# The projection stage of a concat kernel (S4D convolution beside full attention): the seeds' work requested in small pieces between projections

## The chip, the cores and the metric

The kernel runs on one core of one Trainium2 chip, as one launch. The metric is the device time of that launch in microseconds; the median of three runs stands for the kernel.

## What is computed

Two results of shape 1 x 2048 x 448 are put side by side. The first is an S4D state-space convolution: a kernel K of length 2048 for each of 448 channels, from 256 complex modes each, convolved with u. The second is 16-head attention without a mask, with heads of 28.

```python
# A
dt = exp(log_dt); A = -exp(log_A_real) + 1j * A_imag; C = (C_real + 1j * C_imag) * dt[:, None]
P = exp((A * dt[:, None])[:, :, None] * pos[None, None, :])          # 448 x 256 x 2048
K = 2.0 * einsum("dn,dnl->dl", C, P).real
y = irfft(rfft(u_t, 2 * L) * rfft(K, 2 * L), 2 * L)[:, :, :L];  a = y + u * D_skip
# B
q, k, v = split(x @ wqkv);  p = softmax(q @ k.T * 28 ** -0.5);  b = (p @ v) @ wo
out = concatenate([a, b], axis=-1)
```

## The kernel before

The program has three stages.

**The projection stage** (0 to 206 us). The rows of x come in four chunks c of 512. For each chunk `transposes` turns x with TensorE (PE) into four pairs `xh`, `xl` (the value rounded to the matmul's format, by ScalarE (ACT), and the rest, by VectorE (DVE)). Then come twelve projections: eight of q and k (`qk_proj`, one for each of four groups of heads and each of the two) and four of v (`v_proj`); the last chunk has its v first. A projection is twelve matmuls into one of three PSUM buffers `pm`, taken in turn. `project()` issues one projection and then the evacuation of the one before: for q and k ACT writes the high half of `hl`, DVE the low half, and SyncE (SP) stores both; for k of the first two chunks ACT and DVE also form `kb`, and POOL a part of `dhl`. An evacuation of v is ACT's alone.

Between the projections stands work that has nothing to do with them: **the seeds** of the convolution, eight of them (`seeds(o)`, 56 of the 448 channels each). A seed has thirteen steps: `load` (four DMAs), `exp_a` and `times_dt` (ACT), `turn` (eight transposes on PE, a copy on ACT), `phases` (three short and one long instruction on DVE, one long on POOL), `reduce` (two long ones on DVE), `sines` (three long ones on ACT), `sizes` (one long on ACT) with `g_base` (POOL), `places` with the factors `fa` and `e_base` (DVE; POOL), `e3` and `g_first` (DVE, 6 and 9 instructions), the factors `fb` with `e5` and `g_copies` (DVE; POOL; ACT), and two stores. A long instruction has 128 x 1232 elements.

The steps go into slots: step i of seed o into slot 4o + i (`SP` = 4), `load` two slots early. There are 41 slots; the 48 projections are spread evenly over the first `PW` = 37, so that about 1.3 projections are requested, then one slot's steps in whole, then 1.3 projections again:

```python
for t in range(n_stage):
    while work and n_work - len(work) < n_work * (t + 1) / PW:
        project()
    for f in slots[t] + ahead.get(t, []):
        f()
```

After slot 36 the last evacuation is requested and then the loads of the stage to come; the last four slots, seed 7's end, follow.

In this stage nothing is kept in program order (`KEPT["p"]` is empty): the order of requests gives priorities, from which the framework's scheduler makes each engine's instruction order when the program is built. At run time each engine follows its fixed order.

**The bridge** (206 to 260 us): the first loads of k (`khat`), q (`qhat`) and v for attention, and the row maxima of the first unit.

**The main stage** (from 260 us): scores, exponentials and products with v, with the rest of the convolution in between, in an order written out by hand (`ORDER`), which the scheduler keeps.

Every engine instruction is issued through the wrapper `Kept`, so the profile gives line 75 for all of them; they are told apart by their tiles. In the seeds `tri` holds the phases (`r`), sines (`sn`) and sizes (`mg`); `pn` is the turned input in PSUM; `qhat` and `sg` are also the seeds' results; `px` is a PSUM buffer for products.

Of the kernel before, what the change touches and what calls it, by code (L numbers as in the profile page):

```python
# [8 lines left out]
F32 = mybir.dt.float32  # L9
# [3 lines left out]
ALU = mybir.AluOpType  # L13
# [10 lines left out]
HG = H // G  # L24
CQ = 512
NQ = L // CQ
# [64 lines left out]
def body(ctx, tc, a, out):  # L91
# [117 lines left out]
    with ExitStack() as st:  # L209
# [102 lines left out]
        def seeds(o):  # L312
# [23 lines left out]
            def phases():  # L336
                tri = t_p.tile([128, 3, LV, NH], F32, name="tri", bufs=2)
                q["r"], q["sn"], q["mg"] = r, sn, mg = tri[:, 0], tri[:, 1], tri[:, 2]
                t0, k0, im = sn[:, 0, :], sn[:, 1, :], q["ps"][:, 1].rearrange("p b h e -> p (b h e)")
                vec.tensor_scalar(k0, im, MAGIC, None, op0=ALU.add)  # L340
                vec.scalar_tensor_tensor(t0, k0, MAGIC, im, op0=ALU.subtract, op1=ALU.subtract)
                vec.tensor_scalar(t0, t0, 0.5, -0.5, op0=ALU.min, op1=ALU.max)
                mul(vec, r, lb(t0), kb)
                mul(pol, mg, lb(q["tr"]), kb)

            def reduce():
                vec.tensor_scalar(q["sn"], q["r"], MAGIC, MAGIC, op0=ALU.add, op1=ALU.subtract)
                vec.tensor_tensor(q["r"], q["sn"], q["r"], ALU.subtract)

# [29 lines left out]

            def g_first():  # L380

                c0 = q["ps"][:, 2:4].rearrange("p c b h e -> p c (b h e)")
                px = ps_x.tile([128, CQ], F32, name="px")
                c1, x_ = (px[:, i:i + 2 * NH].rearrange("p (c n) -> p c n", c=2) for i in (0, 2 * NH))
                g4_ = lambda e: q["sg"][:, :, :F_Z - F_G].rearrange("p b (c h e) -> p c b h e", c=2, e=4)[:, :, :, :, e]
                bh = lambda t: t.rearrange("p c (b h) -> p c b h", h=16)
                zr = lambda k: q["r"][:, 6 + k, :][:, None, :].to_broadcast([128, 2, NH])
                tt = vec.tensor_tensor
                for k, src, e, dst in ((0, c0, 1, bh(c1)), (1, c0, 2, g4_(2)), (1, c1, 3, g4_(3))):
                    tt(g4_(e), bh(src), bh(zr(k)), ALU.mult)  # L390
                    tt(x_, src[:, ::-1], q["gz"][:, k], ALU.mult)
                    tt(dst, g4_(e), bh(x_), ALU.add)
                q["c"] = c0, c1
# [5 lines left out]

            def factors(i, k, p_, n_):  # L400
                zz, mg = q["zz"], q["mg"]
                mul(vec, zz[:, i:i + 3, :, 0, :], vk(mg, k), vk(q["r"], k))
                mul(vec, zz[:, i:i + 3, :, p_, :], vk(mg, k), vk(q["sn"], k))
                for k in range(i, i + 3):
                    act.activation(zz[:, k, :, n_, :], zz[:, k, :, p_, :], AF.Copy, scale=-1.0)

            def cmul(e, dst, s0, n, wr, wi, conj):

# [4 lines left out]
                br, bi = (w_[:, :, :, None].to_broadcast([128, BO, 16, n]) for w_ in (wr, wi))  # L413
                for c in range(2):
                    mul(e, dst[c], s0[c], br)
# [4 lines left out]
            e8 = lambda *i: sl(q["e8"], *i)  # L420
            e3 = lambda: cmul(vec if o % 8 < E3 else pol, e8(3, 4), e8(1, 2), 1, q["e8"][:, :, 0, :, 2], q["e8"][:, :, 1, :, 2], False)
            e5 = lambda: cmul(pol, e8(5, 8), e8(1, 4), 3, q["e8"][:, :, 0, :, 4], q["e8"][:, :, 1, :, 4], False)
# [3 lines left out]
            def load():  # L426
                if o not in nats:
                    load_nat(o)
                q["nat"] = nats.pop(o)
            dts = lambda *r: [lambda i=i: times_dt(i) for i in r]  # L430
            fa, fb = lambda: factors(0, 3, 2, 1), lambda: factors(3, 8, 1, 2)
            return [[load], [exp_a] + dts(1, 2, 3), dts(0), [turn], [phases], [reduce], [sines], [sizes, g_base],
                    [places, fa, e_base], [e3, g_first], [fb, e5, g_copies], [put_g], [put_e]]

# [59 lines left out]

        work = []
        for c in range(NQ):
            jobs = [lambda c=c, s=s, g=g: qk_proj(c, s, g) for g in range(G) for s in (1, 0)]
            v_jobs = [lambda c=c, t=t: v_proj(c, t) for t in range(4)]
# [8 lines left out]
        for o in range(NO):  # L507
            for i, st_ in enumerate(stages[o]):
                slots[max(SP * o + (i or -2), 0)] += st_
        slots[1].insert(0, turn_dt)  # L510
        pend, n_work = [], len(work)
# [7 lines left out]
        def project():  # L519
# [4 lines left out]
            if e:  # L524
                pend.append(e)

        for t in range(n_stage):
            while work and n_work - len(work) < n_work * (t + 1) / PW:
                project()
            for f in slots[t] + ahead.get(t, []):  # L530
                f()
            if t + 1 == PW:
                project()
                wst.close()
                k0_p = pool(k0_st, "k0_p", side="right")
                for j in range(HG):
                    load_k(0, j, k0_p, nc.scalar if j < 2 else nc.sync)
                load_q(1)
                for c in range(NQ):
                    load_v(0, c)  # L540
        xst.close()
# [569 lines left out]
```

## Time and profile before

| | us |
|---|---|
| median of 3 runs (lowest, highest) | 1343.49 (1342.39, 1343.78) |
| the profiled execution | 1344.13 |
| its span, first to last instruction | 1342.4 |
| TensorE (PE), busy in the span | 1247.8 (93%) |
| VectorE (DVE) | 994.4 (74%) |
| ScalarE (ACT) | 953.5 (71%) |
| GpSimd (POOL) | 838.6 (62%) |

The shares are means over stages with different limits, so a change to one stage is read in that stage. Each row of the stretches gives the length, then the busy time and number of instructions of PE, of its weight loads (PEld), of DVE, ACT and POOL, then the granted TensorE clock, the share of the DMA engines and GB/s. A row of the chain of waits gives start, length and what the end waited for. A row of waits reads: who waited, for whom, in total, how often, the longest. A row of the timeline gives start, length, engine, tiles (out<-in), shape, and in brackets the idle time before it with what ended it. A row of the groups gives tiles, shapes and count, then busy time and the mean of one in ns, then idle time before. An engine named with a q (ACTq, SPq) is its sequencer, which issues DMAs.

### The profile page before, as it was taken

The numbers are of one execution on the slowest core, as the hardware profiler recorded it, in microseconds if no ns is written. First come the engines' busy times: TensorE is split into PE (matmuls) and PEld (weight loads), VectorE is DVE, ScalarE is ACT, GpSimd is POOL, SyncE is SP. The second block draws the span as 40 slices with busy tenths as digits, with TensorE's granted clock in tenths as the row PEclk, the third lists the DMA queues.
The fourth block names the chain that finished last, engine by engine and source line by source line (L and its number), as shares of the span: only waits on it lengthen the run. The fifth ranks groups of instructions, "written<-read, shape, count | busy, mean of one in ns | idle before, by whom it ended". The sixth has DMA issues, their size and how long they took to land.

```text
span 1342.4 us, 33143 instructions
## 1 busy us (share of the span) xinstructions
PE 1247.8 (93%) x12625; PEld 706.7 (53%) x12625; DVE 994.4 (74%) x2138; ACT 953.5 (71%) x2067; POOL 838.6 (62%) x705
## 2 busy tenths in 40 slices
PE   7879885899999999999999999999998899998998
PEld 5657762355555555555555555555554445544433
DVE  5897786877777777787788888988886757757311
ACT  4876762488888788888888888888885556645552
POOL 3685681187878877878889989989983202112221
PEclk9879886899999999999999999999998999999999
DMA  6677669626765556478633314641424444635476
GB/s 196 209 257 260 216 213 290 194 67 146 174 151 122 111 148 173 124 171 222 173 89 85 97 47 92 147 99 47 115 79 144 142 119 169 201 131 190 147 189 174
DMA packets 200088, 205.36 MB, mean 153 GB/s; under 512 B 95992, under 2 KB 158520, under 8 KB 197880
## 3 DMA queue, kind: packets, MB, share of 16 engines
q1 hardware_dynamic: 199544, 201.13, 54.0%
q10 hardware_dynamic: 384, 2.10, 0.5%
q8 instruction: 100, 1.64, 0.5%
q14 instruction: 60, 0.49, 0.1%
HBM read 120.73 MB, written 82.18 MB: 151 GB/s over the span
## 4 chain that ended last, share of the span: by engine, by line
PE 70%; DVE 13%; ACT 6%; DMA 4%; POOL 3%; issue 2%; SPq 1%; ACTq 0%; DVEq 0%; POOLq 0%
PE pm L75 39%; PE po L75 16%; PE pss L75 15%; DVE mx L75 2%; DVE tri L75 2%; ACT p L75 2%; DVE p L75 2%; DVE pr L75 1%; POOL qhat L75 1%; DMA khat<-k 1%; DVE sg L75 1%; DVE px L75 1%; DVE qhat L75 1%; ACT tri L75 1%; DMA q<-hl 1%
## 5 line engine op out<-in xcount | busy, mean ns | idle before, releaser
L75 ACT ACTIVATE p<-pss 128x512 f32<-128x512 f32 x1024 | 562.0, 612 | 142.1 <-PE pss L75 137.7
L75 PE MATMUL pss<-qhat,khat 128*128 128x512 f32 x1024 | 406.3, 403 | 7.0 <-ACT p L75 4.3
L75 DVE TENSOR_REDUCE mx<-pm 128x1 f32<-128x512 f32 x500 | 321.7, 684 | 117.7 <-PE pm L75 113.4
L75 PE MATMUL pm<-khat,qhat 128*128 128x512 f32 x749 | 328.5, 442 | 15.7 <-DVE mx L75 10.9
L75 POOL TENSOR_TENSOR e<-e,sdb 128x256 f32<-128x256 f32 x168 | 201.8, 1201 | 147.0 <-ACT e L75 138.1
L75 PE MATMUL po<-p,v 128*32 128x512 f32 x2048 | 272.4, 599 | 0.0
L75 POOL TENSOR_TENSOR e<-e,eu 128x256 f32<-128x256 f32 x168 | 248.2, 1478 | 13.2
L75 PEld LDWEIGHTS pm<-khat,qhat 128*128 128x128 f32 x749 | 142.6, 191 | 211.7 <-ACT p L75 43.6
L75 PEld LDWEIGHTS pss<-qhat,khat 128*128 128x128 f32 x1024 | 191.2, 189 | 64.1 <-ACT p L75 27.5
L75 DVE CUSTOM_DVE_ANT_0 rl<-pm,rl 128x512 f32<-128x512 f32 x249 | 171.7, 690 | 61.8 <-ACT rl L75 58.0
L75 POOL TENSOR_TENSOR eu<-e,sdb 128x256 f32<-128x256 f32 x168 | 202.0, 1202 | 0.0
L75 ACT ACTIVATE rl<-pm 128x512 f32<-128x512 f32 x249 | 151.5, 609 | 20.8 <-PE pm L75 18.3
L75 DVE TENSOR_TENSOR g<-g,zg 128x128 f32<-128x128 f32 x392 | 162.1, 414 | 4.2 <-ACT zg L75 0.8
L75 POOL TENSOR_TENSOR p<-pr,pr 64x448 f32<-64x448 f32 x32 | 40.9, 1277 | 197.4 <-DVE pr L75 186.4
L75 PE MATMUL pm<-kdif,qhat 128*128 128x512 f32 x249 | 101.6, 408 | 2.4 <-DMA v<-v 1.3
L75 DVE TENSOR_TENSOR zg<-g,zg 128x128 f32<-128x128 f32 x224 | 88.0, 393 | 5.1
L75 PEld LDWEIGHTS pm<-e,g 128*32 128x32 f32 x3584 | 57.4, 110 | 41.5 <-DVE mx L75 18.2
L75 PE MATMUL pm<-xh,wh 112*128 112x512 f32 x128 | 57.8, 456 | 20.9 <-DVE hl L75 9.7
L75 PE MATMUL pm<-e,g 128*32 128x64 f32 x3584 | 73.2, 222 | 0.0
L75 ACT ACTIVATE y<-pm 128x448 f32<-128x448 f32 x48 | 26.3, 548 | 65.6 <-PE pm L75 33.3
L75 PEld LDWEIGHTS po<-p,v 128*32 128x32 f32 x2048 | 56.0, 110 | 22.8 <-issue 18.3
L75 ACT ACTIVATE ub<-pm 128x224 f32<-128x224 f32 (+1 forms) x96 | 38.7, 448 | 39.4 <-PE pm L75 38.3
(137 smaller groups left out, 1575.1 us busy)
## 6 DMA issues: line engine op xcount, KB each, us to landing
sdb<-sd SPq DMA_DIRECT2D x56, 336.0 KB
qhat<-q SPq DMA_DIRECT2D x64, 256.0 KB
khat<-k SPq DMA_DIRECT2D x56, 256.0 KB
sd<-sg SPq DMA_DIRECT2D x8, 1456.0 KB
k<-hl SPq DMA_DIRECT2D x16, 512.0 KB
q<-hl SPq DMA_DIRECT2D x16, 512.0 KB
mw<-in_mw SPq DMA_DIRECT2D x16, 512.0 KB
sd<-qhat SPq DMA_DIRECT2D x8, 896.0 KB
```

The source lines that it names most:

```text
L75: i = f(*args, **kw)
```

## The change

The slots stay, but they are flattened into one queue of (weight, function). The weight is a constant for the DVE time of the piece, in us; steps with little or no DVE work have weight 0. Steps are cut: `phases` gives up its long instructions to `turns`; `reduce`, `e3` and the factors come in two parts, `g_first` in three. Each projection has an amount `took` of DVE time of its own: 0.7 for an evacuation of q or k, 1.1 where `kb` is formed, 0 for v, and 2.0 more where a chunk's transposes come. All weights and amounts together, divided by 48, give `each`; after every projection `due` grows by `each - took`, and pieces are taken from the queue while the next one's weight is not above `due`. A piece of weight 0 is taken at once. What is left in the queue after the 48th projection, and the slots from 37 on, follow as before. The instructions themselves are the same.

```diff
--- before.py
+++ after.py
@@ -340,12 +340,17 @@
                 vec.tensor_scalar(k0, im, MAGIC, None, op0=ALU.add)
                 vec.scalar_tensor_tensor(t0, k0, MAGIC, im, op0=ALU.subtract, op1=ALU.subtract)
                 vec.tensor_scalar(t0, t0, 0.5, -0.5, op0=ALU.min, op1=ALU.max)
-                mul(vec, r, lb(t0), kb)
-                mul(pol, mg, lb(q["tr"]), kb)
-
-            def reduce():
-                vec.tensor_scalar(q["sn"], q["r"], MAGIC, MAGIC, op0=ALU.add, op1=ALU.subtract)
-                vec.tensor_tensor(q["r"], q["sn"], q["r"], ALU.subtract)
+                q["t0"] = t0
+
+            def turns():
+                mul(vec, q["r"], lb(q["t0"]), kb)
+                mul(pol, q["mg"], lb(q["tr"]), kb)
+
+            def reduce(i):
+                if i == 0:
+                    vec.tensor_scalar(q["sn"], q["r"], MAGIC, MAGIC, op0=ALU.add, op1=ALU.subtract)
+                else:
+                    vec.tensor_tensor(q["r"], q["sn"], q["r"], ALU.subtract)
 
             def sines():
                 act.activation(q["sn"], q["r"], AF.Sin, scale=TWO_PI)
@@ -377,19 +382,21 @@
                 mul(pol, gz[:, :, 0], q["mg"][:, 6:8, :], q["sn"][:, 6:8, :])
                 act.activation(gz[:, :, 1], gz[:, :, 0], AF.Copy, scale=-1.0)
 
-            def g_first():
+            def g_first(i):
 
                 c0 = q["ps"][:, 2:4].rearrange("p c b h e -> p c (b h e)")
-                px = ps_x.tile([128, CQ], F32, name="px")
+                if i == 0:
+                    q["px"] = ps_x.tile([128, CQ], F32, name="px")
+                px = q["px"]
                 c1, x_ = (px[:, i:i + 2 * NH].rearrange("p (c n) -> p c n", c=2) for i in (0, 2 * NH))
                 g4_ = lambda e: q["sg"][:, :, :F_Z - F_G].rearrange("p b (c h e) -> p c b h e", c=2, e=4)[:, :, :, :, e]
                 bh = lambda t: t.rearrange("p c (b h) -> p c b h", h=16)
                 zr = lambda k: q["r"][:, 6 + k, :][:, None, :].to_broadcast([128, 2, NH])
                 tt = vec.tensor_tensor
-                for k, src, e, dst in ((0, c0, 1, bh(c1)), (1, c0, 2, g4_(2)), (1, c1, 3, g4_(3))):
-                    tt(g4_(e), bh(src), bh(zr(k)), ALU.mult)
-                    tt(x_, src[:, ::-1], q["gz"][:, k], ALU.mult)
-                    tt(dst, g4_(e), bh(x_), ALU.add)
+                k, src, e, dst = ((0, c0, 1, bh(c1)), (1, c0, 2, g4_(2)), (1, c1, 3, g4_(3)))[i]
+                tt(g4_(e), bh(src), bh(zr(k)), ALU.mult)
+                tt(x_, src[:, ::-1], q["gz"][:, k], ALU.mult)
+                tt(dst, g4_(e), bh(x_), ALU.add)
                 q["c"] = c0, c1
 
             def g_copies():
@@ -397,28 +404,29 @@
                     for e in range(2):
                         act.activation(q["g4"][:, :, c, :, e], q["c"][e][:, c].rearrange("p (b h) -> p b h", h=16), AF.Copy)
 
-            def factors(i, k, p_, n_):
+            def factors(i, k, p_, n_, imag):
                 zz, mg = q["zz"], q["mg"]
-                mul(vec, zz[:, i:i + 3, :, 0, :], vk(mg, k), vk(q["r"], k))
+                if not imag:
+                    return mul(vec, zz[:, i:i + 3, :, 0, :], vk(mg, k), vk(q["r"], k))
                 mul(vec, zz[:, i:i + 3, :, p_, :], vk(mg, k), vk(q["sn"], k))
                 for k in range(i, i + 3):
                     act.activation(zz[:, k, :, n_, :], zz[:, k, :, p_, :], AF.Copy, scale=-1.0)
 
-            def cmul(e, dst, s0, n, wr, wi, conj):
+            def cmul(e, dst, s0, n, wr, wi, conj, cs=(0, 1)):
 
                 if e is nc.vector:
                     x_ = ps_x.tile([128, CQ], F32, name="px")[:, :BO * 16 * n].rearrange("p (b h e) -> p b h e", h=16, e=n)
                 else:
                     x_ = s_p.tile([128, BO, 16, 4], F32, name="x_e")[:, :, :, :n]
                 br, bi = (w_[:, :, :, None].to_broadcast([128, BO, 16, n]) for w_ in (wr, wi))
-                for c in range(2):
+                for c in cs:
                     mul(e, dst[c], s0[c], br)
                     mul(e, x_, s0[1 - c], bi)
                     e.tensor_tensor(dst[c], dst[c], x_, ALU.add if (c == 0) == conj else ALU.subtract)
 
             sl = lambda t, i0, i1: [t[:, :, c, :, i0:i1] for c in range(2)]
             e8 = lambda *i: sl(q["e8"], *i)
-            e3 = lambda: cmul(vec if o % 8 < E3 else pol, e8(3, 4), e8(1, 2), 1, q["e8"][:, :, 0, :, 2], q["e8"][:, :, 1, :, 2], False)
+            e3 = lambda c: cmul(vec if o % 8 < E3 else pol, e8(3, 4), e8(1, 2), 1, q["e8"][:, :, 0, :, 2], q["e8"][:, :, 1, :, 2], False, (c,))
             e5 = lambda: cmul(pol, e8(5, 8), e8(1, 4), 3, q["e8"][:, :, 0, :, 4], q["e8"][:, :, 1, :, 4], False)
             put_e = lambda: nc.sync.dma_start(sd_d[o][:, :, :F_G].rearrange("b p f -> p b f"), q["se"])
             put_g = lambda: nc.sync.dma_start(sd_d[o][:, :, F_G:].rearrange("b p f -> p b f"), q["sg"])
@@ -428,9 +436,13 @@
                     load_nat(o)
                 q["nat"] = nats.pop(o)
             dts = lambda *r: [lambda i=i: times_dt(i) for i in r]
-            fa, fb = lambda: factors(0, 3, 2, 1), lambda: factors(3, 8, 1, 2)
-            return [[load], [exp_a] + dts(1, 2, 3), dts(0), [turn], [phases], [reduce], [sines], [sizes, g_base],
-                    [places, fa, e_base], [e3, g_first], [fb, e5, g_copies], [put_g], [put_e]]
+            fa, fb = ([(0.75, lambda a_=a_, i=i: factors(*a_, i)) for i in range(2)] for a_ in ((0, 3, 2, 1), (3, 8, 1, 2)))
+            rd, e3s = ([(w_, lambda i=i, f=f: f(i)) for i in range(2)] for w_, f in ((1.5, reduce), (1.2, e3)))
+            gs = [(1.5, lambda i=i: g_first(i)) for i in range(3)]
+            free = lambda *fs: [(0.0, f) for f in fs]
+            return [free(load), free(exp_a, *dts(1, 2, 3)), free(*dts(0)), free(turn), [(0.75, phases), (1.4, turns)], rd,
+                    free(sines), free(sizes, g_base), free(places) + fa + free(e_base), e3s + gs, fb + free(e5, g_copies),
+                    free(put_g), free(put_e)]
 
         xh, xl = {}, {}
 
@@ -492,8 +504,10 @@
                 nc.sync.dma_start(v_d[c][:, :, t], vs.rearrange("p (g h) e -> p g (h e)", g=G))
             return evac
 
-        work = []
+        work, took = [], []
+        VJ = [range(8, 12)] * (NQ - 1) + [range(4)]
         for c in range(NQ):
+            took += [2.0 * (not i) + (0.0 if i in VJ[c] else 1.1 if c < 2 and i % 2 == 0 else 0.7) for i in range(12)]
             jobs = [lambda c=c, s=s, g=g: qk_proj(c, s, g) for g in range(G) for s in (1, 0)]
             v_jobs = [lambda c=c, t=t: v_proj(c, t) for t in range(4)]
             jobs = v_jobs + jobs if c == NQ - 1 else jobs + v_jobs
@@ -507,7 +521,7 @@
         for o in range(NO):
             for i, st_ in enumerate(stages[o]):
                 slots[max(SP * o + (i or -2), 0)] += st_
-        slots[1].insert(0, turn_dt)
+        slots[1].insert(0, (0.4, turn_dt))
         pend, n_work = [], len(work)
 
         ahead = collections.defaultdict(list)
@@ -523,21 +537,32 @@
                 pend.pop(0)()
             if e:
                 pend.append(e)
-
-        for t in range(n_stage):
-            while work and n_work - len(work) < n_work * (t + 1) / PW:
-                project()
-            for f in slots[t] + ahead.get(t, []):
+        for t, fs in ahead.items():
+            slots[t] += [(0.0, f) for f in fs]
+
+        queue = collections.deque(p for sl_ in slots[:PW] for p in sl_)
+        each = (sum(w_ for w_, _ in queue) + sum(took)) / n_work
+        due = 0.0
+        for n in range(n_work):
+            project()
+            due += each - took[n]
+            while queue and queue[0][0] <= max(due, 0.0):
+                w_, f = queue.popleft()
+                due -= w_
                 f()
-            if t + 1 == PW:
-                project()
-                wst.close()
-                k0_p = pool(k0_st, "k0_p", side="right")
-                for j in range(HG):
-                    load_k(0, j, k0_p, nc.scalar if j < 2 else nc.sync)
-                load_q(1)
-                for c in range(NQ):
-                    load_v(0, c)
+        while queue:
+            queue.popleft()[1]()
+        project()
+        wst.close()
+        k0_p = pool(k0_st, "k0_p", side="right")
+        for j in range(HG):
+            load_k(0, j, k0_p, nc.scalar if j < 2 else nc.sync)
+        load_q(1)
+        for c in range(NQ):
+            load_v(0, c)
+        for sl_ in slots[PW:]:
+            for _, f in sl_:
+                f()
         xst.close()
         more = [lambda: ps_t.tile([128, CQ], F32, name="pt")] * 2 + [w_tile] * 3
         for i in range(16):
```

## The prediction

> **What bounds the kernel now.** I read the span in stretches first, because the change touches one stage only.
>
> ```profile
> core 0: us, PE busy (x) PEld busy (x) DVE busy (x) ACT busy (x) POOL busy (x), PEclk, DMA share, GB/s
> 0.00:15.00 15.00, 7.20 (x23) 5.42 (x24) 4.40 (x7) 5.87 (x10) 5.06 (x19) 1.00 0.87 235
> 15.00:206.00 191.00, 158.98 (x684) 126.93 (x682) 159.22 (x281) 130.06 (x259) 127.31 (x138) 0.89 0.68 227
> 206.00:242.00 36.00, 20.86 (x49) 10.56 (x49) 23.64 (x51) 9.32 (x18) 2.04 (x2) 0.72 1.05 282
> 260.00:1343.00 1083.00, 1046.02 (x11836) 556.65 (x11836) 792.15 (x1767) 802.81 (x1772) 704.17 (x546) 0.99 0.51 134
> ```
>
> The projection stage is 0 to 206. From 260 on PE is 97% busy (1046.02 of 1083) with an order written by hand: the change does not reach it. The chain of waits says how the one turns into the other:
>
> ```profile
> 196.22 7.33 PE pm L75 x24
> 203.72 1.19 ACTq L75
> 205.01 0.69 ACT hl L75
> 205.70 0.52 ACTq L75
> 206.36 7.29 DMA khat<-k
> 213.72 11.02 DMA q<-hl
> 224.76 8.20 DMA khat<-k
> 232.98 9.03 DMA v<-v
> 242.01 0.77 PE pm L75 x2
> ```
>
> The last projections (196.22) are evacuated at 205.01 to 205.70, and then 36 us of transfers follow at a DMA share of 1.05, until 242.01. These transfers carry the same bytes in both kernels. So one microsecond at the last evacuation is one microsecond of the total; the seeds' work counts only where it delays that evacuation.
>
> In 15 to 206 VectorE (DVE) works 159.22 of 191 us, 83%, as much as PE (158.98). But PE's figure holds slow matmuls:
>
> ```profile
> 33.67 0.40 PE L75 MATMUL pm<-xl,wh 112*128 112x512 f32 x1
> 33.91 0.40 PE L75 MATMUL pm<-xh,wh 112*128 112x512 f32 x1
> 57.06 2.00 PE L75 MATMUL pt<-ident,xn 128*112 128x128 f32 x8 [2.80 <-DVE xl L75]
> 59.28 0.63 PE L75 MATMUL pm<-xh,wl 112*128 112x512 f32 x1
> 59.71 0.63 PE L75 MATMUL pm<-xl,wh 112*128 112x512 f32 x1
> 82.65 0.80 PE L75 MATMUL pm<-xh,wh 112*128 112x512 f32 x1 [5.32 <-DVE hl L75]
> 94.69 0.80 PE L75 MATMUL pm<-xh,wh 112*128 112x512 f32 x1 [4.31 <-DVE kb L75]
> ```
>
> Start to start a matmul of 512 columns takes 0.24 us when PE ran without a break (33.67 to 33.91) and 0.43 us after an idle time of 2.80 us (59.28 to 59.71). At 0.234 a projection of 12 takes 2.81 us, the 32 of q and k 90 us, and even with the 16 of v, taken as long, 135 of the 206. PE waits for DVE; DVE is the engine to count.
>
> What DVE waits for, and PE:
>
> ```profile
> DVE hl L75 <- ACT hl L75: 10.4, 7, 2.1
> DVE sg L75 <- ACT tri L75: 6.7, 10, 2.3
> DVE qhat L75 <- POOL qhat L75: 3.4, 4, 1.9
> DVE xl L75 <- ACT xh L75: 2.7, 2, 1.8
> PE pm L75 <- DVE hl L75: 13.8, 6, 5.3
> PE pm L75 <- DVE kb L75: 6.9, 4, 4.3
> PE pt L75 <- DVE xl L75: 5.4, 2, 2.8
> ```
>
> DVE idles 191 - 159.22 = 31.8 us. DVE's own work is the same list of instructions in both kernels, so the end of the stage moves by the change of this idle time and by nothing else of the first order. A third of it (10.4) is DVE standing at an evacuation that PE and ACT have not delivered, at the same time as PE stands for DVE elsewhere: the two alternate.
>
> **The change, part by part.** *Splitting* (phases/turns, the two halves of `reduce`, `e3`, the factors, three parts of `g_first`) adds no instruction: these were separate instructions before. Only `px` is one buffer held over three pieces. Cost 0, as no engine gets work.
>
> *The new dispenser* orders the requests; the scheduler then makes each engine's order. I counted that order on DVE in both builds, up to the last evacuation. Two prices are needed:
>
> ```profile
> L75 DVE TENSOR_TENSOR tri<-tri,pw 128x1232 f32<-128x1232 f32 x8 | 15.1, 1883 | 0.1
> L75 DVE TENSOR_TENSOR tri<-tri 128x1232 f32<-128x1232 f32 x8 | 14.8, 1852 | 0.1
> L75 DVE TENSOR_SCALAR tri<-tri 128x1232 f32<-128x1232 f32 x8 | 8.8, 1098 | 0.1
> ```
>
> The 24 long instructions are 38.7 us, 1.61 each; the other 257 of the stretch are (159.22 - 38.7)/257 = 0.47 each. With these, an estimate of DVE's work in the four quarters of the 32 q and k evacuations (eight of each chunk c):
>
> ```
> DVE instructions (short+long), us    c=0        c=1        c=2        c=3
> before                               62+3 34.0  72+9 48.3  57+6 36.5  75+6 44.9
> after                                74+6 44.4  67+6 41.2  61+7 39.9  64+5 38.1
> longest run between two evacuations
> inside a chunk, before               21+0  9.9  19+1 10.5  13+0  6.1  14+0  6.6
> inside a chunk, after                11+3 10.0  17+1  9.6  15+0  7.1  11+0  5.2
> ```
>
> So the quarters do become even, mostly because the seeds begin earlier: 10 us of work move into the first chunk. The runs inside a chunk do not become shorter: the scheduler gathers the small pieces again, and 10 us between two evacuations stand in chunk 0 now as well. (The first run of chunk 0, 21+0, is start-up arithmetic, the same in both.) That run is worth a PE stall: two freed buffers are 2 x 2.81 = 5.6 us of PE work against 10, as the 5.32 and 4.31 stalls of before show. Because DVE is the bound, such a stall costs nothing unless DVE afterwards stands for PE.
>
> Where DVE stands for PE today is at the seams of the chunks, where PE must wait for the last `xl` and then is slow:
>
> ```profile
> 116.32 1.29 DVE L75 TENSOR_TENSOR xl<-pt,xh 112x512 fp32r<-112x512 f32 x2
> 117.53 0.54 DVE L75 TENSOR_TENSOR sg<-sg,px 128x224 f32<-128x224 f32 x1
> 120.13 0.75 DVE L75 SCALAR_TENSOR_TENSOR hl<-pm,kones,hl 128x512 fp32r<-128x512 f32 x1 [2.06 <-ACT hl L75]
> 122.84 0.69 DVE L75 TENSOR_TENSOR hl<-pm,hl 128x512 fp32r<-128x512 f32 x1 [1.96 <-ACT hl L75]
> ```
>
> At this seam (c=1 to 2) the order before has one short instruction between the last `xl` and the first evacuation and none between first and second. After, it has seven and two, that is 3.3 and 0.9 us of cover instead of 0.5 and 0: the 2.06 goes, and 0.9 of the 1.96. At the seam c=0 to 1, two short ones become two short and a long one, 1.6 us more cover; a wait of the same kind (up to the 2.1 in the waits table) shrinks by at most that. Together 2.06 + 0.9 + 1.6 = 4.6 us saved.
>
> *Earlier seeds.* In the first chunk DVE has gaps, in which nothing else was asked for:
>
> ```profile
> 30.00:57.00 27.00, 20.98 (x107) 17.23 (x105) 23.20 (x36) 22.47 (x44) 17.68 (x17) 0.98 0.64 206
> ```
>
> It works 23.20 of these 27 us. More work to choose from saves between zero and 3.8 us; I take 2, since the first seed still needs its loads and ScalarE's scaling, which have not moved in front of anything.
>
> *The end.* After the first evacuation of chunk 3, DVE's order holds 26 short instructions instead of 43 short and 3 long: 12.2 us instead of 25. PE needs for the five projections that no buffer holds yet 5 x 2.81 = 14.1 us, and ACT's and DVE's last evacuation 0.69 each (the rows at 205.01 and 122.84), 15.4 in all. So the end, until now bounded by DVE, becomes bounded by PE, and 15.4 - 12.2 = 3.2 us of the gain are lost as DVE idle time. Between 0 (if PE is already ahead) and 6 (if PE enters it slow).
>
> *SyncE and POOL.* The loads of the next seeds' `nat` are now queued ahead of the first stores of k and q; a store that waits holds its `hl` buffer, and ScalarE's next evacuation waits for it. I take 0, as stores have two buffers, and keep 3 us for the range. POOL's instructions keep their order per seed. DVE and POOL disturb each other:
>
> ```profile
> 75.73 2.29 DVE L75 TENSOR_TENSOR tri<-tri,pw 128x1232 f32<-128x1232 f32 x1
> 76.68 3.44 POOL L75 TENSOR_TENSOR tri<-tr,pw 128x1232 f32<-128x1232 f32 x1
> 126.04 1.44 DVE L75 TENSOR_TENSOR tri<-tri,pw 128x1232 f32<-128x1232 f32 x1
> ```
>
> The same DVE instruction took 2.29 us beside POOL's and 1.44 at 126.04. The Trainium skill, SBUF — State Buffer, section "SBUF: two separate sides", calls the shared pair of ports an exclusive lock, with the later one blocked for the whole instruction; that speaks against spreading DVE's work over time in which POOL is busy. By that rule these two would not overlap at all; the trace shows both lengthened instead. For the 16 long tensor-tensor instructions (mean 1.87), all at 2.29 would be +6.7 us, all at 1.44 -6.9. POOL is busy 67% of the stage either way, so I take 0.
>
> The sum: -4.6 - 2 + 3.2 = -3.4 us. The profiled execution took 1344.13 (span 1342.4 and 1.7 around it), 0.64 above the median 1343.49, to which the sum is added: 1340.1 us. (What a measurement of this kernel can tell from no change is about 0.2%, 2.7 us.)
>
> On PE's slow matmuls the Trainium skill, TensorE: Matmul & The Clock Gate, section "Part 1: The HAM clock gate", gives half rate after at least one idle window of about 3.4 us. Here an idle time of 2.80 was enough; by the page only the 5.32 and 4.31 stalls would be followed by slow matmuls. The sum has no term for it; it is why the seams cost DVE as much as they do.
>
> **The rivals.**
> *It does more than the seams* (chance 0.17). If pieces between projections keep PE supplied throughout, all DVE waits for evacuations (10.4), for `xh` (2.7) and the 2 at the start go, less the 3.2 at the end: -11.9, 1331.6 us. For it: the quarters are even. Against: the runs of 10 us.
>
> *It does not do what it says* (0.15). The scheduler undoes the interleaving, gains at the seams equal new waits elsewhere: 1343.5. For it: the lower half of the table.
>
> *The factors come right behind the sines* (0.22), the slower side. Before, sines, sizes and factors were requested one slot of 48/37 projections apart; now the sines, the sizes and the factors follow in the queue with no weighted piece between them. DVE is a queue in order: while a factor waits for ScalarE's cosine, the evacuations behind it wait, and PE for them. Today the wait is 6.7 us over eight seeds, 0.84 each; at the longest seen, 2.3, for each of eight it is 18.4, +11.7. Less the 4.6 - 3.2 + 2 of above: +8.3, 1351.8 us. It decides from 0.84 + 3.4/8 = 1.27 us a seed, where the gain is gone. Against it: in the built order the scheduler still places other work there.
>
> *The early seeds hurt the first chunk* (0.13), slower too: ScalarE's sines and POOL's products stand in front of the first evacuations and stores, the 3 us of the store buffers and a POOL overlap at the upper end (+6.7) with half the gain: 3 + 6.7 - 1.7 = +8.0, 1351.5 us.
>
> **How the numbers follow.** The forecast, -3.4, has 0.33; with its unknown terms (early seeds 0 to 3.8, end 0 to 6) its own range is 1336 to 1343, so I count 0.30 of it beyond 0.2% and 0.03 within. Faster: 0.30 + 0.17 = 0.47. Same: 0.15 + 0.03 = 0.18. Slower: 0.22 + 0.13 = 0.35. The range takes in the greater part of the second case and most of the last two, whose stated prices are near their upper ends: 1330 to 1352.
>
> **What would show it.** Right: the last evacuation near 202 instead of 205.7, the transfers behind it still 36 us; DVE busy near 159 in the stage and its waits for ACT's `hl` down from 10.4 to 5 or 6; no 2 us wait after the last `xl` of chunk 1; a new DVE wait for `hl` in the last 15 us. PE stalls of 4 to 5 us in chunk 0 that were not there. Wrong: `sg <- ACT tri` well above 6.7 (the factors), `ACT hl <- DMA` in the first 50 us (stores), DVE busy above 163 (POOL), or a last evacuation at 196 or earlier.

## The result, and the profile after

The changed kernel takes 1358.12 us (median of 4 runs, 1357.83 to 1361.35), the kernel before 1342.94 (4 runs, 1335.02 to 1343.78): ratio 1.0126, 95% interval 1.0100 to 1.0152. It is slower by 15 us; 1340.1 was forecast, with 1330 to 1352 as the range. The profiled execution took 1357.99 us (span 1356.2, before 1342.4: +13.8).

I cut the span at three events that both traces have: the end of the last evacuation of q and k on DVE (before 207.7, after 217.1), the first exponential of attention (`p<-pss`, before 260.0, after 273.4), and the end. The stage is 9.4 us longer, the bridge between the two events 4.0 (52.3 to 56.4), attention 0.4.

The stage, first in the kernel before, cut at the evacuations 7, 15, 17, 23, 24, 28 and 31 (the last) of its 32, counted from 0. Columns: window, its length, then busy time of each engine.

```profile
core 0: us, PE busy (x) PEld busy (x) DVE busy (x) ACT busy (x) POOL busy (x), PEclk, DMA share, GB/s
15.00:49.13 34.13, 29.75 (x140) 22.66 (x138) 26.22 (x59) 24.61 (x49) 14.61 (x16) 1.00 0.60 197
49.13:104.06 54.93, 41.69 (x167) 33.15 (x168) 49.90 (x82) 40.27 (x83) 42.63 (x46) 0.81 0.66 226
104.06:123.53 19.47, 16.88 (x78) 13.82 (x77) 12.88 (x28) 11.18 (x29) 11.34 (x15) 0.91 0.78 253
123.53:151.41 27.88, 23.57 (x111) 19.04 (x110) 25.75 (x37) 18.70 (x36) 17.22 (x20) 0.94 0.66 234
151.41:180.67 29.26, 26.65 (x123) 22.66 (x123) 21.49 (x36) 21.86 (x41) 21.02 (x23) 0.91 0.57 181
180.67:199.49 18.82, 16.40 (x55) 12.68 (x54) 16.75 (x30) 12.47 (x25) 15.04 (x15) 0.77 0.84 284
199.49:207.66 8.17, 4.05 (x18) 2.92 (x16) 7.89 (x17) 1.57 (x3) 7.02 (x10) 0.91 0.98 334
```

The same cuts in the kernel after, same columns:

```profile
15.00:57.35 42.35, 35.48 (x139) 26.54 (x138) 37.84 (x74) 28.80 (x59) 23.10 (x21) 0.84 0.49 162
57.35:110.92 53.57, 40.48 (x187) 32.34 (x185) 46.30 (x75) 39.07 (x80) 39.16 (x48) 0.93 0.68 229
110.92:126.96 16.04, 15.99 (x63) 13.71 (x64) 13.14 (x25) 11.31 (x24) 10.45 (x7) 0.80 0.70 234
126.96:164.32 37.36, 28.75 (x129) 22.57 (x127) 27.99 (x44) 23.16 (x45) 23.04 (x29) 0.91 0.66 221
164.32:194.45 30.13, 24.15 (x104) 20.29 (x105) 26.26 (x43) 20.04 (x39) 22.29 (x21) 0.83 0.61 194
194.45:208.89 14.44, 11.83 (x51) 9.26 (x50) 5.52 (x10) 6.64 (x16) 3.69 (x9) 1.00 0.90 307
208.89:217.07 8.18, 4.20 (x18) 3.03 (x17) 7.97 (x17) 1.68 (x3) 5.77 (x6) 0.96 0.88 261
```

Length less DVE's busy time is DVE's idle time in each stretch:

```
stretch             chunk 0   chunk 1   seam 1-2  rest of 2  seam 2-3  ev. 25-28  29-31   sum
DVE idle, before      7.9       5.0       6.6       2.1        7.8       2.1       0.3    31.8
DVE idle, after       4.5       7.3       2.9       9.4        3.9       8.9       0.2    37.1
difference           -3.4      +2.2      -3.7      +7.2       -3.9      +6.8      -0.1    +5.3
```

The gains are there, 11 us in three stretches. Two stretches take 14 us back, chunk 1 another 2. The waits of the changed kernel from 15 to 215 (what waited and for whom; us in total, times, longest):

```profile
DVE hl L75 <- ACT hl L75: 13.0, 9, 3.5
DVE sg L75 <- ACT tri L75: 7.6, 7, 3.7
...
ACT hl L75 <- DMA k<-hl: 4.8, 2, 2.7
```

The last row is 2.5 us in the kernel before, none of it in the end stretch. The timeline shows one place for each of the two losses (start, length, in brackets the idle time ahead of it and what ended it):

```profile
124.74 0.73 DVE L75 SCALAR_TENSOR_TENSOR hl<-pm,kones,hl 128x512 fp32r<-128x512 f32 x1
126.29 0.67 DVE L75 TENSOR_TENSOR hl<-pm,hl 128x512 fp32r<-128x512 f32 x1
128.08 1.28 ACT L75 ACT_TABLE_LOAD   x1
129.37 1.23 ACT L75 ACTIVATE tri<-tri 128x1232 f32<-128x1232 f32 x1
130.64 1.40 DVE L75 TENSOR_TENSOR sg<-tri 128x336 f32<-128x336 f32 x2 [3.68 <-ACT tri L75]
...
202.89 0.69 ACT L75 ACTIVATE hl<-pm,kones 128x512 fp32r<-128x512 f32 x1 [2.11 <-DMA k<-hl]
203.61 0.75 DVE L75 SCALAR_TENSOR_TENSOR hl<-pm,kones,hl 128x512 fp32r<-128x512 f32 x1 [3.54 <-ACT hl L75]
207.41 0.69 ACT L75 ACTIVATE hl<-pm,kones 128x512 fp32r<-128x512 f32 x1 [2.69 <-DMA k<-hl]
208.14 0.75 DVE L75 SCALAR_TENSOR_TENSOR hl<-pm,kones,hl 128x512 fp32r<-128x512 f32 x1 [2.69 <-ACT hl L75]
```

At the seam the two evacuations (124.74, 126.29) carry no bracket: the waits of 2.06 and 1.96 are gone. The next thing in DVE's queue is a factor, and it stands 3.68 us for ScalarE's table load and exponential. In the end stretch DVE stands for ACT, and ACT for a store of k to release its `hl` buffer.

Then the chain of waits behind the last evacuation:

```profile
215.73 0.74 DVE hl L75
217.41 1.32 SPq L75
218.77 11.68 DMA qhat<-q
230.59 1.19 PE pt L75 x2
...
261.88 0.60 DVE rl L75
262.47 1.22 DVE mx L75 x3
...
273.44 1.09 ACT p L75 x2
```

The chain before ran over `khat`, a store of q and `v`. This one runs over the first q that attention needs: the last two of its four parts are issued from 217.41, the chain waits for them until 230.45, and the first maximum `pt<-kdif,qhat` begins at 230.59 (before: 217.20). The row maxima, 1.81 us on DVE for each block, start only then. SyncE's queue says why:

```profile
216.50 0.36 SPq L75 DMA_DIRECT2D k<-hl  x1
216.90 0.47 SPq L75 DMA_DIRECT2D sd<-sg  x1
217.41 2.41 SPq L75 DMA_DIRECT2D qhat<-q  x2
```

The loads stand behind the store of the last k, which waits for the last evacuation of k. Before, they were issued ahead of that store:

```profile
210.11 0.80 SPq L75 DMA_DIRECT2D qhat<-q  x2
211.00 0.38 SPq L75 DMA_DIRECT2D k<-hl  x1
```

### The profile page after: what moved, and what is told of

The parts are those of the page before. It is cut to its first block, busy times and chain, and to the rows that moved or that the text cites. A ratio compares the mean times of both kernels' runs of the same rounds, so it can differ in the third digit from the quotient of the medians.

```text
span 1356.2 us, 33136 instructions
## 1 busy us (share of the span) xinstructions
PE 1250.3 (92%) x12625; PEld 706.7 (52%) x12625; DVE 999.0 (74%) x2138; ACT 954.0 (70%) x2067; POOL 837.8 (62%) x705
## 4 chain that ended last, share of the span: by engine, by line
PE 70%; DVE 14%; ACT 6%; POOL 3%; issue 3%; DMA 3%; SPq 0%; ACTq 0%; DVEq 0%; POOLq 0%
PE pm L75 39%; PE po L75 16%; PE pss L75 15%; DVE mx L75 3%; DVE p L75 2%; ACT p L75 2%; DVE pr L75 1%; POOL qhat L75 1%; DVE tri L75 1%; DVE qhat L75 1%; DVE rl L75 1%; DVE sg L75 1%; DVE px L75 1%; DMA qhat<-q 1%; DVE hl L75 1%
## 5 line engine op out<-in xcount | busy, mean ns | idle before, releaser
L75 PEld LDWEIGHTS pm<-e,g 128*32 128x32 f32 x3584 | 57.3, 109 | 41.4 <-DVE mx L75 18.2
```

What stands on the lines that cost most here:

```text
L75: i = f(*args, **kw)
```

## The experiments

All in one table. "Ratio" is against the kernel before on the same chip (its medians there 1342.56, 1342.71, 1343.08). The last four columns are from each profiled execution: end of the last evacuation, DVE's busy time up to there, start of the first row maximum, start of the first exponential. From the first exponential to the end these executions take between 1076.4 and 1084.5 us (1082.4 before, 1082.8 after), so a total does not follow the stage and the bridge to the microsecond. (For e10 the busy time is left out, since row maxima stand ahead of its last evacuation.)

```
run                     median   ratio   95% interval      last ev.  DVE busy  1st max.  1st exp.
before                  1342.94                              207.7    165.3     217.2     260.0
after                   1358.12  1.0126  1.0100 to 1.0152    217.1    169.4     230.6     273.4
e1_loads_back           1346.77  1.0032  1.0012 to 1.0051    212.7    167.4     213.4     263.5
e2_lags                 1345.93  1.0032  1.0013 to 1.0050    210.3    167.8     220.7     263.7
e3_whole_steps          1349.54  1.0056  1.0035 to 1.0078    209.5    164.8     223.2     265.9
e4_cut_only             1343.16  1.0006  0.9988 to 1.0025    209.3    165.4     218.1     261.1
e5_q_back               1355.83  1.0110  1.0078 to 1.0143    220.7    168.2     221.9     271.7
e6_kdif_back            1350.35  1.0072  1.0038 to 1.0106    212.9    167.0     225.1     266.7
e7_loads_and_lags       1351.80  1.0084  1.0052 to 1.0116    211.3    164.5     225.4     268.6
e9_before_loads_early   1344.72  1.0020  0.9998 to 1.0043    209.5    166.5     206.8     261.3
e10_end_46              1347.88  1.0045  1.0027 to 1.0063    226.2              211.1     264.1
e11_end_44              1360.34  1.0133  1.0099 to 1.0167    222.9    159.8     210.3     274.9
e12_late_start          1348.04  1.0036  1.0020 to 1.0053    210.0    160.8     222.5     263.9
e13_redrawn             1360.85  1.0141  1.0116 to 1.0167    218.5    168.5     232.2     274.8
```

**Cut the steps, keep the old dispenser.** The changed kernel with the loop of before:

```diff
-        for n in range(n_work):
-            project()
-            due += each - took[n]
-            ...
+        for t in range(n_stage):
+            while work and n_work - len(work) < n_work * (t + 1) / PW:
+                project()
+            for _, f in slots[t]:
+                f()
```

> The steps cut as in the change, but given out by slots as before it. Theory A: the same as before the change within 0.2% (1340 to 1346), as no request moves. Rival D (the cutting does the damage): slower by 5 us or more, 1348 to 1358.

1343.16 us, the same as before (the interval allows a cost of up to 0.25%), with each stretch of the stage within 0.6 us of before but the last, which is 1.7 us longer. Cutting alone costs nothing that these runs can see; the loss needs the new dispenser.

**Keep the dispenser, do not cut.** The pieces of a step are joined again (`phases` with `turns`, `rd`, `e3s` with `gs`, `fb`, and `places` with `fa`):

```diff
+            whole = lambda ps: [(sum(w_ for w_, _ in ps), lambda: [f() for _, f in ps])]
-            return [..., [(0.75, phases), (1.4, turns)], rd, ...
+            return [..., whole([(0.75, phases), (1.4, turns)]), whole(rd), ...
```

> The changed kernel with whole steps as pieces (phases with turns 2.15, reduce 3.0, places with factors 1.5, e3 with g_first 6.9, second factors 1.5): the amounts still decide when, but nothing is cut. Theory A (the cutting is harmless and useless, the moved request times do the damage): within 4 us of the changed kernel, 1354 to 1362. Rival D (the cutting itself does the damage, since the scheduler mixes the pieces of two seeds): 8 to 15 us faster than the changed kernel, near 1345.

1349.54: 8.6 us faster than with the pieces. DVE is busy 164.8 us instead of 169.4 and idle 44.7 instead of 47.6 up to the last evacuation; the first maximum is 13.7 us behind that evacuation as in the changed kernel (13.5). So under this dispenser the small pieces are worse than whole steps, by more than half of the whole loss.

**The loads ahead of attention.** `ahead` holds 8 loads of `kdif` and the first two of q. In the changed kernel they are entries of the queue, and come after projections 36 to 47 (`kdif`) and 48 (q); before, after 36 to 45 and 46, 47. The first run asks for them at the projections of before:

```diff
+        early = collections.defaultdict(list)
         for t, fs in ahead.items():
-            slots[t] += [(0.0, f) for f in fs]
+            early[min(-(-n_work * (t + 1) // PW), n_work)] += fs
         ...
+            for f in early[n + 1]:
+                f()
```

> The changed kernel, but the eight loads of kdif and the two of the first q leave the weighted queue and are requested after the same projections as before the change (36 to 47 instead of 36 to 48). Theory A (three causes: the first q arrives late, factors right behind the sines, DVE instructions stretched): the loads alone are worth the bridge, so 3 to 5 us come back of the 15, and the first attention transfers land about 4 us earlier; the last evacuation moves by less than 2 us. Rival B (everything is the projection stage itself): within 1.5 us of the changed kernel. Rival C (the stores at the end wait behind the kdif loads): 6 to 9 us come back, because the two waits of ScalarE for k stores near 203 and 207 go.

1346.77, 11.4 us faster than the changed kernel, more than any of the three expectations allowed for. Its SyncE queue, first maximum and first exponential:

```profile
206.37 2.11 SPq L75 DMA_DIRECT2D qhat<-q  x2
214.57 0.38 SPq L75 DMA_DIRECT2D k<-hl  x1
...
213.43 0.76 PE L75 MATMUL pt<-kdif,qhat 128*128 128x512 f32 x1 [4.60 <-issue]
...
263.52 1.08 ACT L75 ACTIVATE p<-pss 128x512 f32<-128x512 f32 x2
```

The loads of q are ahead of the last store of k again, the first maximum comes 0.7 us behind the last evacuation instead of 13.5, and the bridge is 50.8 instead of 56.4. The stage is shorter too, by 4.4. Which load does which, in two runs with one kind each:

```diff
+            if t < A0 + 2 * HG:           # e5: only the loads of q go to `early`; e6: >= in place of <, only those of kdif
+                slots[t] += [(0.0, f) for f in fs]
+            else:
+                early[min(-(-n_work * (t + 1) // PW), n_work)] += fs
```

> The changed kernel; only the two loads of the first q are requested where they were before the change (after projections 46 and 47), the kdif loads stay in the weighted queue. In SyncE's built order the last two parts of q then stand ahead of the last k store, as before the change. Theory A: the bridge from the last evacuation to the first attention exponential falls from 56.3 to 50 to 53 us, the last evacuation stays at 217 within 2 us; in all 4 to 6 us faster than the changed kernel's 1358, so 1352 to 1354. Rival B (the kdif loads among the last stores did it): within 2 us of 1358. Rival E (the schedule is merely redrawn): the last evacuation moves by 4 us or more.

> The changed kernel; only the eight kdif loads are requested where they were before the change, the first q stays in the weighted queue, its last two parts behind the last k store in SyncE's order. Theory A: the bridge stays at 55 to 57 us; the last evacuation comes 2 to 5 us earlier, since one of ScalarE's two waits for k stores near 203 and 207 goes: 1353 to 1356. Rival B: 1347 to 1349, all that taking both back gained. Rival E (a redrawn schedule): no relation to the bridge.

With q alone the bridge is 51.0, but the last evacuation 3.6 us later still (220.7): 1355.83. In that build DVE's and ACT's orders at the end are others, and DVE's evacuation at 219.37 stands 5.04 us for ACT's. With `kdif` alone the last evacuation is at 212.9, 4.2 us earlier, with the bridge at 53.9: 1350.35. So q behind the last store costs the bridge some 5 us. For `kdif` less is shown than the 4.2 us: the stretch of the evacuations 25 to 28 idles 6.45 us instead of 8.92 (6.46 in e1), and ScalarE waits there for one store of k (2.32 us in e6) instead of two. That is 2.5 us. DVE's busy time is 2.4 us shorter in e6 and the idle time elsewhere 0.7 longer, and why is not shown. The totals show the two parts less cleanly, since e5's last evacuation moved as well.

The opposite, in the kernel before: the loads one or two slots earlier (`A0, A1 = 24, 33` for `26, 34`).

> The kernel before the change with A0, A1 = 24, 33 instead of 26, 34: the kdif loads two slots and the first q one slot earlier; the order on SyncE then has all four parts of q ahead of the last two k stores and of seed 6's sd store. Theory A: the first row maximum starts earlier than 217.2 (the first khat has landed by about 212), the bridge shortens by 1 to 4 us: 1339 to 1342. Rival F (the bridge is held by the bytes of khat and v, not by the first q): the same within 0.2%, 1341 to 1345.

The first maximum begins at 206.8 instead of 217.2, 10 us earlier, and the first exponential not at all (261.3): 1344.72, 1.0020 with an interval that touches 1. Counted from the last evacuation, which came 1.8 us later here (209.5), the bridge is 51.8 against 52.3. Early q is worth next to nothing where the other branch of the bridge ends last.

The table gives the rule of the bridge: the first exponential comes at the later of last evacuation + 51 us (a chain that begins with transfers of `khat`) and first maximum + 43 us (the row maxima). For before that is 258.7 against 260.2 (measured 260.0); after, 268.1 against 273.6 (273.4); e1 263.7 against 256.4 (263.5); e7 262.3 against 268.4 (268.6). All rows but e10 agree to 1.6 us. It was read off these runs, so it is a description of them; e9 speaks for the two branches most plainly.

**Distance between sines and factors.** An empty piece of weight 1.5 ahead of the sizes and one ahead of the factors:

```diff
-   free(sines), free(sizes, g_base), free(places) + fa + free(e_base), ...
+   free(sines), [(1.5, lambda: None)] + free(sizes, g_base), [(1.5, lambda: None)] + free(places) + fa + free(e_base), ...
```

> The changed kernel with an empty piece of weight 1.5 ahead of sizes and another ahead of places, so that sines, sizes and factors are again asked for after different projections. Theory A: the 3.7 us wait of DVE for ScalarE's exponentials near 130 goes, PE's stalls around it too, 3 to 6 us faster than the changed kernel; the seeds then end a little later. Rival B (the waits behind the sines are not the cause, what counts is that the last seeds come later): no gain or 1 to 4 us slower, since the empty pieces push the last seed back further.

1345.93, 12.2 us faster than the changed kernel. The last evacuation is at 210.3 with 42.5 us of DVE idle, as before (42.4). The heavier queue also moved q ahead of the last store of k (first maximum 10.4 us behind the last evacuation), so of the gain 3.0 are the bridge's and 6.8 the stage's. But the gain of the stage is not the wait that the empty pieces were meant for. DVE's waits from 15 us to the last evacuation in this run:

```profile
DVE sg L75 <- ACT tri L75: 11.2, 7, 3.2
DVE hl L75 <- ACT hl L75: 5.0, 3, 3.1
```

The wait for the sines and sizes is longer in sum than in the changed kernel (7.6); its longest is 3.2 us instead of 3.7. The wait at the evacuations is what fell, from 13.0.

Lags and loads together:

> The changed kernel with both repairs: all ten loads where they were, and the empty pieces of weight 1.5 ahead of sizes and places. Theory A: bridge near 51 us, last evacuation near 210, so 1340 to 1344, equal to the kernel before or slightly faster. Rival E (each of the two alone only redrew a bad schedule): 1345 to 1348, no better than either alone.

1351.80: not the sum, but worse than either. The stage is nearly as short as with lags (211.3), but q is now behind two stores of the seeds on SyncE, and the bridge is 57.3. The repairs are not additive.

**The pace.** The same pieces, all asked for two or four projections before the end:

```diff
-        each = (sum(w_ for w_, _ in queue) + sum(took)) / n_work
+        each = (sum(w_ for w_, _ in queue) + sum(took)) / (n_work - 2)     # e11: - 4
```

> The changed kernel with `each` made for 46 projections instead of 48, so that the queue runs empty two projections earlier: seed 7's sines, seed 6's stores and the loads of the first q are requested after projection 45 (46 to 48 before the change, 48 with it). Theory A (the change pushes the last seeds and the loads to the end): the last evacuation comes at 207 to 211 instead of 217 and the bridge falls to 51 to 54 us: 1341 to 1348. Rival G (the evened first chunks, with DVE's longer instructions, cost it): 1353 to 1360, as they are as even as in the changed kernel.

> The same with 44: everything in the queue is requested by projection 43, nothing but projections remains at the end. Theory A: not slower than with 46, 1338 to 1348; the end becomes bound by PE and ScalarE's evacuations (at least 2.81 us for each of the last projections). Rival G: 1353 to 1362, as the work is packed still closer before the end.

With two, 1347.88. The scheduler puts the last evacuations behind row maxima (226.2), and attention does not wait for them: the first exponential is at 264.1. With four, 1360.34. DVE's busy time is the shortest of all (159.8), and it idles 63.1 us up to the last evacuation:

```profile
DVE hl L75 <- ACT hl L75: 24.9, 10, 6.7
```

The seeds' work is done too early and nothing is left to cover the last projections. And the other way, a start with 8 us of debt:

```diff
-        each = (sum(w_ for w_, _ in queue) + sum(took)) / n_work
-        due = 0.0
+        each = (sum(w_ for w_, _ in queue) + sum(took) - (-8.0)) / n_work
+        due = -8.0
```

> The changed kernel with 8 us of debt at the start (the sum stays): the first seed's phases are requested after projection 5 instead of 2 (7 before the change), the last ones still at 48. Theory A: no gain, 1354 to 1361, because the end is as it is in the changed kernel. Rival G (the early seeds crowd the first chunk): 5 us or more faster, 1345 to 1353.

1348.04, 10 us faster than the changed kernel, which is what was expected if the early seeds do harm. The idle time is not less (49.2 against 47.6); it is DVE's busy time that is, 160.8 against 169.4. So it does not wait less; its instructions are shorter, of which more below.

**Is the changed kernel an unlucky order?** The amounts `took` are altered by a hair (1.1 to 1.05, 0.7 to 0.72), which gives the scheduler another order of a few instructions.

> The changed kernel with two amounts changed by a hair (1.1 to 1.05 and 0.7 to 0.72), so that a few requests swap places and DVE's built order differs in two dozen lines. Theory A: as the changed kernel, 1355 to 1361. Rival E (any edit redraws the schedule, and the changed kernel is an unlucky draw): several us away, 1343 to 1353.

1360.85, with nearly the same last evacuation (218.5), DVE busy time (168.5) and bridge (56.3). So the loss does not hang on one order of a few instructions; this is one redrawing, not a sample of them.

None of these is faster than the kernel before. With the loads where they were, even amounts still cost 0.32% (0.12 to 0.51).

## Why the prediction was wrong

*"These transfers carry the same bytes in both kernels. So one microsecond at the last evacuation is one microsecond of the total."* This step failed: +4.0 us. The bytes are the same, but not their places in SyncE's queue. The diff moves `ahead` into the queue of pieces, and I counted the loads of `nat` and the stores there but not these ten. I also read the chain as the only way: the branch over q and the maxima ended within 2 us of it in the kernel before. e1, e5 and e9 show it.

*DVE's own work is the same, so only idle time counts.* Failed: up to the last evacuation DVE is busy 4.1 us longer with the same 290 instructions. This is the term "DVE and POOL, 0" with its bounds of -6.9 and +6.7. The groups of DVE instructions from 15 to 218, before:

```profile
L75 DVE TENSOR_TENSOR sg<-tri 128x336 f32<-128x336 f32 x32 | 22.1, 698 | 6.7 <-ACT tri L75 6.7
L75 DVE TENSOR_TENSOR tri<-tri,pw 128x1232 f32<-128x1232 f32 x8 | 15.1, 1883 | 0.1
L75 DVE TENSOR_TENSOR qhat<-qhat 128x112 f32<-128x112 f32 x16 | 9.7, 631 | 3.4 <-POOL qhat L75 3.4
```

and after:

```profile
L75 DVE TENSOR_TENSOR sg<-tri 128x336 f32<-128x336 f32 x32 | 25.0, 800 | 7.6 <-ACT tri L75 7.6
L75 DVE TENSOR_TENSOR qhat<-qhat 128x112 f32<-128x112 f32 x16 | 13.5, 856 | 5.4 <-POOL qhat L75 5.1
L75 DVE TENSOR_TENSOR tri<-tri,pw 128x1232 f32<-128x1232 f32 x8 | 13.1, 1632 | 0.0
```

I had priced the long instructions, and the dearest of those became shorter (15.1 to 13.1). The short ones grew: 9.7 to 13.5 and 22.1 to 25.0. The last section shows that it is POOL that they stand for.

*The seams, -4.6.* Right in kind. The predicted seam gave 3.7 (I took 3.0), and the one between chunks 2 and 3, which I had not listed, 3.9. The seam between 0 and 1 gave 1.4 of the 1.6: the wait of its first evacuation fell from 2.11 (at 65.33) to 0.71 (at 75.10). But the changed kernel has a wait of 2.69 for POOL's `qhat` in the same chunk (at 63.16), and chunk 1 as a whole is 2.2 worse.

*Earlier seeds, -2.* DVE's idle time in chunk 0 fell by 3.4, inside the bounds of 0 and 3.8. But the work that moved there stood for POOL: up to the eighth evacuation DVE's instructions hold 10.6 us above their shortest instead of 6.4, and in the rest of the stage, with less work, 31.3 instead of 29.4 (counted as in the last section). What was gained in idle time was lost again in busy time. This is the POOL part of the rival *the early seeds hurt the first chunk* (0.13); its other part, ScalarE waiting for stores in the first 50 us, did not come. With the start put off (e12) the 10.6 is 8.3, and the sum over the whole stage is 10 us less. That is one run, so it supports the early start as the cause and does not isolate it.

*The end, +3.2.* Wrong in size and in cause: +6.8. It is not PE that DVE waits for but ACT, and ACT waits for a store of k (4.8 us, two times). I had looked for `ACT hl <- DMA` in the first 50 us, where it did not come; it came in the last 15. With `kdif` asked for as before (e6) this stretch idles 2.5 us less; one wait for a store of k stays, and the rest of the 6.8 is open.

*Factors right behind the sines.* I gave this rival 0.22 with 11.7 us over eight seeds. The wait for ACT's `tri` rose from 6.7 to 7.6 only, so as priced it did not happen. But one of them, 3.68 us, stands where the seam's gain was to be kept, and what was gained there is lost within one evacuation. Empty pieces between the two (e2) take 6.8 us off the stage, but with a longer wait for `tri` in sum (11.2), so the 6.8 do not speak for this rival. What in e2's order shortened the waits at the evacuations stays open.

*Splitting, 0.* Right (e4).

In sum: -3.4 was forecast for the stage. It came to +9.4 (idle +5.3, busy +4.1), with +4.0 in the bridge and +0.4 in attention: +13.8.

## What to carry to other kernels

When a dispenser of requests is rewritten, list every DMA that rides in it and find its new place among the stores of an in-order queue: a load behind a store inherits that store's wait. Equal amounts of one engine's work between two events are not equal waits: the work must also lie where its own producers are done (3.68 us of waiting for ScalarE's exponential in one place), and where another engine does not hold it up (some 40 us of DVE's recorded durations here are standing for POOL). And before a chain of waits is taken as the bound, look for a second branch that ends within a few microseconds of it.

## What the runs showed of the hardware

A busy time is not always work. Rows of the changed kernel, DVE and POOL together:

```profile
63.81 2.25 POOL L75 TENSOR_TENSOR tri<-tr,pw 128x1232 f32<-128x1232 f32 x1
64.30 2.95 DVE L75 TENSOR_TENSOR qhat<-qhat 128x112 f32<-128x112 f32 x1
66.01 1.02 POOL L75 TENSOR_TENSOR qhat<-qhat 128x336 f32<-128x336 f32 x1
...
107.86 2.24 POOL L75 TENSOR_TENSOR tri<-tr,pw 128x1232 f32<-128x1232 f32 x1
108.02 2.30 DVE L75 TENSOR_TENSOR qhat<-qhat 128x112 f32<-128x112 f32 x1
111.75 0.35 DVE L75 TENSOR_TENSOR qhat<-qhat 128x112 f32<-128x112 f32 x1
```

The same DVE instruction takes 0.35 us at 111.75, and 2.30 and 2.95 when it begins during a POOL instruction; both times it ends 0.22 us after POOL's (110.10 and 110.32; 67.03 and 67.25). Most of that time it was waiting; in the row at 64.30 a second POOL instruction, begun at 66.01, also went ahead of it. The pair in the prediction reads the same way, with the POOL row that comes before it in the kernel before:

```profile
75.70 1.02 POOL L75 TENSOR_TENSOR qhat<-qhat,x_e 128x336 f32<-128x336 f32 x1
```

DVE's 75.73 began just after this one had begun, which ends at 76.72; 76.72 and DVE's own 1.44 make 78.16, and it ended at 78.02. POOL's 76.68 began under DVE's; 78.02 and POOL's own 2.24 make 80.26, against 80.12 in the trace. So the sentence in the prediction that both are merely lengthened was a misreading: the recorded duration holds the blocked time. The Trainium skill, SBUF — State Buffer, section "SBUF: two separate sides", has whichever of the two starts first keep the shared pair for the whole instruction while the other blocks; among the cases it names is a DVE instruction with two inputs in SBUF against a POOL instruction that reads SBUF. These rows agree.

This also says how large the term is. Take each of DVE's 290 instructions up to the last evacuation, less the shortest with the same tiles and shape in five traces. The sum of these excesses, and the part of it in instructions that begin while a POOL instruction runs:

```
                     before   after   e13    e3    e12
excess, us            35.7     41.9   40.7   35.3   32.1
begun under POOL      33.8     39.8   38.7   33.3   29.8
```

(Neighbouring instructions overlap a little, so the sums move more than the busy times, 165.3, 169.4, 168.5, 164.8 and 160.8.) Nearly all of the excess, and 6.0 of the rise of 6.2, is in instructions that begin under POOL. Who began first decides: over the five traces `sg<-tri` took 496 ns on average without POOL, 507 when POOL began only after it, and 910 when POOL was already running. The evacuation `hl<-pm,hl`, which reads one of its inputs from PSUM, took 682 ns with POOL running and without. So the rise of 4.1 in busy time, which I had put at zero, is DVE standing for POOL, as far as these durations show it. What is not shown is which part of the new order brings the two together more often; that it is lower with whole steps (e3) and with a late start (e12) is all that these runs say.
